# Second products of MoE1 by Strassen's method, with partial sums seeded in PSUM

## The chip, the cores and the metric

The kernel runs on one core of a Trainium2 chip. The core has a matrix engine (TensorE, PE in the rows), a vector engine (VectorE, DVE), an activation engine (ScalarE, ACT), GpSimd (POOL) and SyncE (SP); SP and POOL issue the DMAs here. Operands lie in SBUF, matmuls write into eight PSUM banks. The metric is the device time of one execution in microseconds (us), as the median of several.

## What is computed

```python
kv = einsum('bhsd,bhse->bhde', k, v); out = einsum('bhsd,bhde->bhse', q, kv)
x = out / sqrt(mean(out*out, -1) + 1e-6) * g_norm     # 4608 tokens x 512
r = maximum(x @ w_in, 0); x = (s * (r*r) + b) @ w_out   # MoE1: 512 -> 2048 -> 512
h = x @ w2_in; y = (h / (1 + exp(-1.702*h))) @ w2_out   # MoE2, same sizes
```

All of it is float32.

## The kernel before, in words

The 4608 tokens are nine blocks of T = 512. Every float32 product is made of three matmuls with operands split into a high and a low part (`w` into wh and wl, an activation into xh and xl or gh and gl): wh·xh, wh·xl, wl·xh. A matmul is 128x128 weights on 128x512 values. The low parts are differences on VectorE (`x_lo`, `mlp_g`, `g2_lo`, `go_lo`), the high parts copies on ScalarE.

MoE1 (`m = 0`) does blocks 0 to 2 plainly, interleaved with attention and the preparation of the weights. Then come three pairs of blocks, (3,4), (5,6) and (7,8). Their first products (x @ w_in) go by Strassen's method in Winograd's form: the weights and activations are quartered, and seven products of quarters or sums of quarters replace eight (`first_products`: eight groups of seven products, six matmuls in a product, 336 matmuls). The weight sums (S1 to S4 beside A11 to A22, `OPS`) are made once and kept in DRAM. The second products of these pairs are plain (`second_plain`: 384 matmuls at L569). MoE2 (`m = 1`) has four such pairs, with Strassen's method for both products, and a last plain block.

Products are summed thus in a group (`g1_product`, `g1_sum`): the first goes into PSUM bank a; ScalarE copies it to SBUF (L628); VectorE adds the product in b to the copy (L631), then the one in c (L635), and takes from these the quarters r of the result, with the product in d (L638) and so on: five adds a group. The fifth product goes on in bank a, the seventh in bank d after L638 has read it. Then r is squared (MoE1) or gated: ScalarE makes a sigmoid, VectorE multiplies (L649, L650). MoE1 scales r by s and adds b (`g2_scale`, L670) before it is split.

The order of every engine's instructions is written by hand: `at(slot, fn, ...)` puts a step at a time slot (twelve matmuls, 2.72 us), all steps are sorted by slot, and each step emits its instructions on whatever engines it uses. `attend` is the attention of a block, `x_operands` and `x_sub` (L506) the sums of activations, `w_join`, `s_sums` (L267 to L270), `op_hi`, `op_lo` (L283) and `op_store` the preparation of weight sums.

Of the kernel before, what the change touches and what calls it, by code (L numbers as in the profile page):

```python
# [27 lines left out]
KV = ((-0.5, 2.5), (24.5, 28), (34, 41), (46, 57), (62.5, 66.5), (74, 79), (84, 89))  # L28
# [4 lines left out]
ATT = ((1.5, 2.5, 3.3), (40, 3.5, 4.8), (55, 4, 4.8), (67, 4, 4.8))  # L33
LEAD_G = 3.9
SIDE = (0, 0, 0, 1, 2, 0, 0, 0, 0, 2, 0, 1, 1, 1, 1, 2)
# [49 lines left out]
LEAD = 4  # L85
LAG = 2
G1_ACT = (0, 0, 0, 1.5, 0.2, 1.6, 1.6)
OPS = ("A11", "S2", "S3", "S1", "A12", "A22", "S4", "A21")
PRODUCTS = (("A11", "B11"), ("S2", "T2"), ("S3", "T3"), ("S1", "T1"), ("A12", "B21"), ("A22", "T4"), ("S4", "B22"))

# [17 lines left out]
def kernel(ctx: ExitStack, tc: tile.TileContext, q_h, kv_h, kt, vt, cst,  # L108
# [15 lines left out]

    def new(slots, shape, dtype, name):
        t, n = slots.take(shape, dtype, name)
        where[id(t)] = (slots, n, t)
        return t

    def drop(*tiles):  # L130
        for t in tiles:
            slots, n, _ = where.pop(id(t))
            slots.give(n)
# [6 lines left out]

    def psum(name):
        return new(bank, [P, T], F32, name)
# [6 lines left out]
    g_col = cp.tile([P, 1], F32, name="g_col")  # L149
    eps = cp.tile([P, 1], F32, name="eps")  # L150
# [20 lines left out]
    raws, vals, W = {}, {}, {}  # L171

    def w_load(m, f, which):
        raw = new(big, [P, 512, 2], U32, "raw")
        src = w_raw[m][which]
        nc.sync.dma_start(out=raw.rearrange("p c t -> p (c t)"), in_=src[f * P:(f + 1) * P, :])
        raws[m, f, which] = raw
# [37 lines left out]
    wod = [dp.tile([P, 2, 512], F32, name=f"wod{f}") for f in range(NF)]  # L215
    wsd = [[dp.tile([P, len(OPS), 512], F32, name=f"wsd{m}_{i}") for i in range(NF // 2)] for m in range(2)]
    wo2 = [dp.tile([P, NF // 2, 512], F32, name=f"wo2{name}") for name in OPS]

    def op_place(m, i, which, name):
        return wo2[OPS.index(name)][:, i, :] if which else wsd[m][i][:, OPS.index(name), :]  # L220
# [6 lines left out]
    def wo_store(f):  # L227
        pool.dma_start(out=wod[f], in_=W[0, f, 1].bitcast(F32))

    def wo_load(m, f):  # L230
        w = W[m, f, 1] = new4(F32R, "w")
        if m == 0:
            nc.sync.dma_start(out=w.bitcast(F32), in_=wod[f])
        else:
            for a, name in enumerate(OP_PAIRS[1][f % 2]):
                nc.sync.dma_start(out=w[:, a, :].bitcast(F32), in_=op_place(m, f // 2, 1, name))

    def a_store(f):
        w = W[0, f, 0]
        for c, name in enumerate(OP_PAIRS[0][f % 2]):  # L240
            pool.dma_start(
                out=op_place(0, f // 2, 0, name).rearrange("p (h c) -> p h c", h=2),
                in_=w[:, :, c * 256:(c + 1) * 256].bitcast(F32),
            )

    def w_join(f):
        w = W[0, f, 0]
        q = vals[0, f, 0] = new2(U32, "ca")
        dve.tensor_add(out=q.bitcast(F32), in0=w[:, 0, :].bitcast(F32), in1=w[:, 1, :].bitcast(F32))

        w_spent(f)
# [3 lines left out]
    def w_spent(f):  # L255
        if f in spent:
            drop(W.pop((0, f, 0)))
        spent.add(f)
# [165 lines left out]
    def att_copy(j, p):  # L424
        o_ps, sq = att[j, p]
        o = new2(F32, "oc")
        dve.tensor_copy(out=o, in_=o_ps)
# [69 lines left out]
    def x_lo(src, key, last):  # L497
        hi, lo = xop[key]
        dve.tensor_sub(out=lo, in0=xin[src], in1=hi.bitcast(F32))
        if last:  # L500
            drop(xin.pop(src))
# [9 lines left out]
    def mlp_h(m, j, f, first=0, last=NP):  # L511
# [16 lines left out]
        elif j == NPLAIN - 1:  # L528
            w_spent(f)
# [4 lines left out]
    def mlp_act(m, j, f):  # L534
# [5 lines left out]
        else:  # L540
            act.activation(r, h, AF.Sigmoid, scale=1.702)
            dve.tensor_mul(out=r, in0=h, in1=r)
# [29 lines left out]
    def wo_done(m, f):  # L572
        drop(W.pop((m, f, 1)))
# [25 lines left out]
    def g1_product(m, i, k):  # L599
        op, xname = PRODUCTS[k]  # L600
        n = OPS.index(op)
        w = wl[m, i, n // 2][:, n % 2, :]
        x = xop[m, xname]
# [10 lines left out]
        if k in (1, 3, 5, 6):  # L614
            drop(wl.pop((m, i, {1: 0, 3: 1, 5: 2, 6: 3}[k])))
        if i == NF // 2 - 1 and k == 6:
            for _, name in PRODUCTS:
                drop(*xop.pop((m, name)))

    def r_half(q, i):  # L620
        if i % 2 == 0:
# [3 lines left out]
    def g1_sum(m, i, k):  # L625
        if k == 0:
            st["c1"] = new2(F32, "c1")
            act.activation(st["c1"], st[0], AF.Copy)  # L628
        elif k == 1:
            st["u2"] = new2(F32, "u2")  # L630
            dve.tensor_add(out=st["u2"], in0=st[1], in1=st["c1"])  # L631
            drop(st.pop(1), st.pop("c1"))
        elif k == 2:
            st["u3"] = new2(F32, "u3")
            dve.tensor_add(out=st["u3"], in0=st[2], in1=st["u2"])  # L635
            drop(st.pop(2))
        elif k == 3:
            dve.tensor_add(out=r_half("22", i), in0=st[3], in1=st["u3"])  # L638
        elif k == 5:
            dve.tensor_add(out=r_half("21", i), in0=st[5], in1=st["u3"])  # L640
            drop(st.pop(5), st.pop("u3"))
        elif k == 6:
            dve.tensor_add(out=r_half("12", i), in0=st[6], in1=st["u2"])
            drop(st.pop(6), st.pop("u2"))
            del st[3]

    def gate(r, h):
        t = new2(F32, "t")
        act.activation(t, h, AF.Sigmoid, scale=1.702)  # L649
        dve.tensor_mul(out=r, in0=h, in1=t)  # L650
        drop(t)

    def g1_act(m, i, k):
        if k == 4:
            r = r_half("11", i)
            if m == 0:
                act.activation(r, st[4], AF.Relu)
            else:
                gate(r, st[4])
            drop(st.pop(4))  # L660
            del st[0]
        elif m == 1 and k in (3, 5, 6):
            r = R[{3: "22", 5: "21", 6: "12"}[k], i // 2][:, i % 2, :]
            gate(r, r)

    def r_act(q, n, fn):
        act.activation(R[q, n], R[q, n], fn)  # L667

    def g2_scale(q, n):
        act.activation(R[q, n], R[q, n], AF.Identity, scale=s_col, bias=b_col)  # L670

    def quarter(f, n):
        return ("11", "12", "21", "22")[f % 2 * 2 + n], f // 4, f // 2 % 2

    def g2_hi(m, j, f, n):
        gh, gl = G[m, j, f] = new2(F32R, "gh"), new2(F32R, "gl")
        q, i, half = quarter(f, n)
        act.activation(gh, R[q, i][:, half, :], AF.Copy)  # L678

    def g2_lo(m, j, f, n):  # L680
        gh, gl = G[m, j, f]
        q, i, half = quarter(f, n)
        dve.tensor_sub(out=gl, in0=R[q, i][:, half, :], in1=gh.bitcast(F32))  # L683
        if half:
            drop(R.pop((q, i)))


# [3 lines left out]
    def t_sums(n):  # L691
        t = new4(F32, "t1")
        dve.tensor_sub(out=t, in0=R["12", n], in1=R["11", n])
        dve.tensor_sub(out=R["12", n], in0=R["22", n], in1=t)
        drop(t)
# [384 lines left out]
```

## Time and profile before

| | |
|---|---|
| median of 3 timed runs | 1547.94 us (1547.73 to 1550.01) |
| profiled execution, its own time | 1547.51 us |
| its span, first to last instruction | 1545.6 us |
| TensorE busy | 1530.0 us, 99% |
| VectorE, ScalarE busy | 1062.7 us (69%), 789.6 us (51%) |
| moved by DMA | 392.11 MB, mean 254 GB/s |

The profiled execution is one run with timestamps for each instruction. Busy shares are means over all stages; the stages of the pairs lie, in us from the span's start: pair (3,4) first products 334.7 to 420.9, second 420.9 to 507.9; pair (5,6) 508.0 to 593.8 and to 680.8; pair (7,8) 680.9 to 757.0 and to 844.0; then MoE2, each stage 76 us.

### The profile page before, as it was taken

What the parts mean: (1) busy time and instruction counts of PE and PEld (TensorE: products, weight loads), DVE (VectorE), ACT (ScalarE), POOL (GpSimd) and SP (SyncE); (2) the same over time, 40 slices, a digit from 0 to 9 for tenths busy, and PEclk for the clock granted to TensorE, in tenths of its full rate; (3) what the DMA queues carried; (4) which work ended last, traced back from release to release, by engine and by line L of the source; (5) the groups of instructions that cost most, each with busy time, mean ns of one, the idle gap of its engine ahead of it and who ended that gap; (6) DMA issues with size and microseconds to landing.
All of it is one profiled execution on the core that took longest, in us unless ns stands there. A gap on an engine that the chain in (4) does not pass through costs nothing.

```text
span 1545.6 us, 20632 instructions
## 1 busy us (share of the span) xinstructions
PE 1530.0 (99%) x7368; PEld 1238.4 (80%) x7368; DVE 1062.7 (69%) x1535; ACT 789.6 (51%) x1169; POOL 232.6 (15%) x424
## 2 busy tenths in 40 slices
PE   8999999999999999999999999999999999999998
PEld 5788777877788778888888888888888888888887
DVE  5996366577885677847661889688958795788422
ACT  5997454445893569826871245323522453244221
POOL 1101425512421333221201000000000000000000
PEclk9999999999999999999999999999999999999999
DMA  9635568897896989778865737974797479347930
GB/s 356 206 99 212 197 226 299 281 401 269 305 390 235 325 300 374 273 282 286 295 226 171 249 114 276 357 275 139 266 365 258 148 260 378 126 168 235 374 122 28
DMA packets 125270, 392.11 MB, mean 254 GB/s; under 512 B 17008, under 2 KB 17136, under 8 KB 125168
## 3 DMA queue, kind: packets, MB, share of 16 engines
q1 hardware_dynamic: 93664, 289.18, 53.2%
q0 software_dynamic: 31504, 101.61, 17.8%
q8 instruction: 59, 0.97, 0.2%
q14 instruction: 43, 0.35, 0.1%
HBM read 300.42 MB, written 90.31 MB: 253 GB/s over the span
## 4 chain that ended last, share of the span: by engine, by line
issue 50%; PE 36%; ACT 4%; DMA 4%; POOL 3%; DVE 3%; SPq 0%; POOLq 0%; ACTq 0%; DVEq 0%
PE o L569 18%; PE h L522 6%; PE d L612 3%; PE a L612 3%; PE c L612 1%; PE b L612 1%; PE f L612 1%; POOL out L593 1%; ACT r L667 1%; DMA raw<-in_w_in 1%; DMA kv_in<-in_kv 1%; PE kv L350 1%; PE o_ps L381 1%; DMA qq<-in_q 1%; DMA x0d<-oc 1%
## 5 line engine op out<-in xcount | busy, mean ns | idle before, releaser
L569 PE MATMUL o<-gh,w 128*128 128x512 f32 x1280 | 404.7, 390 | 0.0
L569 PEld LDWEIGHTS o<-gh,w 128*128 128x128 f32 x1280 | 240.2, 188 | 53.8 <-issue 4.0
L740 PE MATMUL o<-gh,wl 128*128 128x512 f32 x896 | 276.5, 389 | 0.0
L569 PE MATMUL o<-gl,w 128*128 128x512 f32 x640 | 249.0, 389 | 0.0
L740 PEld LDWEIGHTS o<-gh,wl 128*128 128x128 f32 x896 | 168.2, 188 | 34.9
L740 PE MATMUL o<-gl,wl 128*128 128x512 f32 x448 | 174.3, 389 | 0.0
L522 PE MATMUL h<-xh,w 128*128 128x512 f32 x512 | 170.7, 395 | 1.9 <-DVE w L211 1.1
L612 PE MATMUL d<-xh,wl 128*128 128x512 f32 x448 | 156.9, 391 | 3.5 <-DVE r L638 3.5
L612 PE MATMUL a<-xh,wl 128*128 128x512 f32 x448 | 156.6, 390 | 0.0
L569 PEld LDWEIGHTS o<-gl,w 128*128 128x128 f32 x640 | 120.1, 188 | 24.5
L522 PEld LDWEIGHTS h<-xh,w 128*128 128x128 f32 x512 | 96.2, 188 | 29.7 <-issue 5.0
L628 ACT ACTIVATE c<-a 128x512 f32<-128x512 f32 x56 | 33.4, 597 | 163.0 <-PE a L612 160.1
L593 POOL DMA_DIRECT2D out<-st x36 | 19.6, 544 | 591.0 <-DVE st L762 467.4
L612 PEld LDWEIGHTS d<-xh,wl 128*128 128x128 f32 x448 | 84.1, 188 | 23.5 <-DVE r L638 5.1
L522 PE MATMUL h<-xl,w 128*128 128x512 f32 x256 | 100.3, 392 | 0.2 <-DVE xl L481 0.2
L612 PEld LDWEIGHTS a<-xh,wl 128*128 128x128 f32 x448 | 84.1, 188 | 20.2 <-issue 2.8
L740 PEld LDWEIGHTS o<-gl,wl 128*128 128x128 f32 x448 | 84.1, 188 | 17.5
L683 DVE TENSOR_TENSOR gl<-r,gh 128x512 fp32r<-128x512 f32 x96 | 65.0, 687 | 33.2 <-ACT gh L678 16.5
L612 PE MATMUL d<-xl,wl 128*128 128x512 f32 x224 | 87.2, 389 | 0.0
L612 PE MATMUL a<-xl,wl 128*128 128x512 f32 x224 | 87.2, 389 | 0.0
L667 ACT ACTIVATE r<-r 128x1024 f32<-128x1024 f32 x84 | 84.5, 1052 | 0.0
L714 ACT ACTIVATE gh<-t 128x1024 fp32r<-128x1024 f32 x48 | 51.0, 1062 | 63.7 <-DVE t L705 58.1
(129 smaller groups left out, 2778.7 us busy)
## 6 DMA issues: line engine op xcount, KB each, us to landing
wl<-wsd SPq DMA_DIRECT2D x168, 512.0 KB, 6.4
wl<-wo2S SPq DMA_DIRECT2D x64, 512.0 KB, 6.2
wsd<-op POOLq DMA_DIRECT2D x96, 256.0 KB, 4.6
w<-wod SPq DMA_DIRECT2D x48, 512.0 KB, 8.1
wl<-wo2A SPq DMA_DIRECT2D x48, 512.0 KB, 4.5
kv_in<-in_kv SPq DMA_DIRECT2D x32, 512.0 KB, 5.7
raw<-in_w_in SPq DMA_DIRECT2D x32, 512.0 KB, 7.9
raw<-in_w_out SPq DMA_DIRECT2D x32, 512.0 KB, 6.2
```

What stands on the lines that cost most here:

```text
L350: pe.matmul(kv[r:r + D, p // 2, h * D:(h + 1) * D], lhsT=kt_, rhs=vt_, start=(p in (opens, opens + 1) and h == 0 and c == 0), stop=False, ...
L381: pe.matmul(att[j, p][0][h * D:(h + 1) * D, o:o + n], lhsT=kvs[b % 4][r:r + D, p // 2, h, :], rhs=qin[j, p // 2][r:r + D, h, o:o + n], sta ...
L522: pe.matmul(h, lhsT=a, rhs=b, start=(n == 0), stop=(n == 3 * NP - 1))
L569: pe.matmul(acc[m, j][c], lhsT=a, rhs=x, start=(f == 0 and n == 0), stop=(f == NF - 1 and n == 2))
L593: pool.dma_start(out=out[c * P:(c + 1) * P, j * T:(j + 1) * T], in_=t)
L612: pe.matmul(o, lhsT=a, rhs=b, start=(first and n == 0), stop=(n == 5), skip_group_check=not first)
L628: act.activation(st["c1"], st[0], AF.Copy)
L667: act.activation(R[q, n], R[q, n], fn)
L683: dve.tensor_sub(out=gl, in0=R[q, i][:, half, :], in1=gh.bitcast(F32))
L714: act.activation(hi, src, AF.Copy)
L740: pe.matmul(so[k, d], lhsT=a, rhs=b, start=(first and n == 0 and i == 0 and e == 0), stop=(n == 3 and i == 1 and e == 2), skip_group_check ...
```

## The change

1. The second products of MoE1's three pairs are done by the method that MoE2 uses (`second_products(0, ...)`, 336 matmuls). The sums of W_out's quarters are prepared and stored like those of W_in. The scale s is applied when results leave PSUM, and b as a constant per output row, b times the column sums of W_out (`col_add`, `col_sums`: four matmuls of one column); `g2_scale` is gone for the pairs.
2. In both MoEs partial sums are formed in PSUM. ScalarE copies a finished bank into another bank (`g1_copy`, `g2_seed`: ub from pa, uc from ub, ob from oa, oc from ob), and matmuls go on accumulating on it without a start flag. pd is copied to SBUF by ScalarE. Two VectorE adds a group remain. `psum()` gives a seed only a bank that matmuls have filled whole. The order of products follows (`G1_PLACE`, `G1_FIRST`, `G2_ORDER`).
3. MoE2's gate is one activation (`Gelu_apprx_sigmoid`) instead of sigmoid and product.
4. Attention's copies out of PSUM (`att_copy`) go to ScalarE for all blocks but 1.
5. The slots (`ATT`: start of a block's attention, gap, and when its scaling begins; `G2`: how many slots ahead of a product its weights are loaded, its sums formed and split) of attention, weights and sums are other numbers (`KV`, `ATT`, `GROUPS`, `SUMS`, `X0`, ...), and all groups of W2_in are prepared before those of W2_out. When the middle-sized tiles run out, a big one is halved.

```diff
-ATT = ((1.5, 2.5, 3.3), (40, 3.5, 4.8), (55, 4, 4.8), (67, 4, 4.8))
+ATT = ((1.5, 2.5, 3.3), (40, 3.5, 4.8), (55.977, 2.5, 5.138), (67, 3.698, 4.378))
...
+G2 = (4.012, 3.247, 2.887, 1.879)
+G2_ORDER = (0, 3, 1, 4, 2, 6, 5)
...
+G1_PLACE = (0, 3, 6, 5, 8, 9, 11)
+G1_FIRST = (0, 2, 6, 1, 3, 9, 11)
...
     def g1_product(m, i, k):
...
-        first = k not in (4, 6)
-        st[k] = psum("abcdefg"[k]) if first else st[0 if k == 4 else 3]
-        o = st[k]
+        if k in (0, 3):
+            st[i, "pa" if k == 0 else "pd"] = psum("pa" if k == 0 else "pd")
+        o = st[i, ("pa", "ub", "uc", "pd", "pa", "uc", "ub")[k]]
...
-                pe.matmul(o, lhsT=a, rhs=b, start=(first and n == 0), stop=(n == 5), skip_group_check=not first)
+                pe.matmul(o, lhsT=a, rhs=b, start=(k in (0, 3) and n == 0), stop=(n == 5), skip_group_check=k not in (0, 3))
...
+    def g1_copy(i, k):
+        if k == 3:
+            t = new2(F32, "c4")
+            act.activation(t, st[i, "pd"], AF.Copy)
+            drop(st[i, "pd"])
+            st[i, "pd"] = t
+            return
+        src, name = (("pa", "ub"), ("ub", "uc"))[k]
+        st[i, name] = psum(name)
+        act.activation(st[i, name], st[i, src], AF.Copy)
+
+    def g1_sum(i, q):
+        a = st[i, "uc" if q == "22" else "ub"]
+        dve.tensor_add(out=r_half(q, i), in0=st[i, "pd"], in1=a)
...
+        act.activation(r, src, AF.Gelu_apprx_sigmoid if m else AF.Relu)
...
+    def g2_seed(k, d):
+        src, name = (("oa", "ob"), ("ob", "oc"))[k]
+        so[name, d] = psum(name)
+        act.activation(so[name, d], so[src, d], AF.Copy)
...
+            act.activation(t, o, AF.Identity, scale=s_col, bias=cb[:, half + d:half + d + 1])
...
+                dve.scalar_tensor_tensor(out=t, in0=o, scalar=s_col, in1=u, op0=ALU.mult, op1=ALU.add)
...
-        base = second_plain(j, seconds[0, j])
+        base = second_products(0, j, seconds[0, j])
...
-        base = second_products(j, seconds[1, j])
+        base = second_products(1, j, seconds[1, j])
```

What stands in an engine's queue at three places, before and after. First ScalarE where the first products of pair (3,4) begin, before (L582 stores the last plain block, L628 is the copy of a's product, L182 and L183 convert MoE2's weights, L390 squares attention):

```order
L582 ACTIVATE st<-o 128x512 x2
L628 ACTIVATE c_3369<-a 128x512
L182 ACTIVATE ca<-raw 128x512
L183 ACTIVATE cu<-raw 128x512
L657 ACTIVATE r<-a 128x512
L182 ACTIVATE ca<-raw 128x512
L183 ACTIVATE cu<-raw 128x512
L390 ACTIVATE sq<-o_ps 128x512 x2
```

The same place in the change (L713 writes a seed, L707 copies pd, L725 takes r out of PSUM, L348 and L234 are weights, L460 attention):

```order
L658 ACTIVATE st<-o 128x512 x2
L348 ACTIVATE op<-s_3506 128x2x256
L348 ACTIVATE op<-s_3507 128x2x256
L713 ACTIVATE ub<-pa 128x512
L707 ACTIVATE c_3585<-pd 128x512
L713 ACTIVATE uc<-ub 128x512
L725 ACTIVATE r<-pa 128x512
L713 ACTIVATE ub<-pa 128x512
L234 ACTIVATE ca<-raw 128x512
L235 ACTIVATE cu<-raw 128x512
L725 ACTIVATE r<-uc 128x512
L460 ACTIVATE sq<-o_ps 128x512
```

Three copies from PSUM stand where one stood, two of them with ub or uc, PSUM banks, as the target.

Second VectorE at the end of the preparation, before (L499 is a low part of an activation operand, L506 a difference of operands, L283 a low part of a weight sum, L631 to L638 the adds of the first group):

```order
L499 TENSOR_TENSOR xl<-x,xh 128x1024
L554 TENSOR_SCALAR g<-r,cst_sb 128x512
L559 TENSOR_TENSOR gl<-g,gh 128x512
L283 TENSOR_TENSOR op<-s_3213,op 128x2x256
L499 TENSOR_TENSOR xl<-x,xh 128x1024
L506 TENSOR_TENSOR x<-x 128x1024
L499 TENSOR_TENSOR xl<-x,xh 128x1024
L580 COPY st<-o 128x512 x2
L499 TENSOR_TENSOR xl<-x,xh 128x1024
L631 TENSOR_TENSOR u_3373<-b,c_3369 128x512
L635 TENSOR_TENSOR u_3395<-c,u_3373 128x512
L638 TENSOR_TENSOR r<-d,u_3395 128x512
```

The same place in the change (L572 and L580 are now the operands, L299 joins a weight of W_out, L337 to L340 sum it, L313 adds to its column sums, L717 is the add of r22):

```order
L337 TENSOR_TENSOR s_3506<-ca 128x256
L338 TENSOR_TENSOR s_3507<-ca 128x256
L339 TENSOR_TENSOR s_3506<-s_3506,ca 128x256
L340 TENSOR_TENSOR s_3507<-ca,s_3506 128x256
L313 TENSOR_TENSOR cs<-cs,s_3506 128x256
L313 TENSOR_TENSOR cs<-cs,s_3507 128x256
L572 TENSOR_TENSOR xl<-x,xh 128x1024
L656 COPY st<-o 128x512 x2
L353 TENSOR_TENSOR op<-s_3506,op 128x2x256
L353 TENSOR_TENSOR op<-s_3507,op 128x2x256
L572 TENSOR_TENSOR xl<-x,xh 128x1024
L717 TENSOR_TENSOR r<-c_3585,uc 128x512
```

W_out's sums stand between the last operands, and of the first group's adds one follows where three did.

Third VectorE in the second stage of pair (3,4), before (L683 makes gl for the plain products, 512 elements wide; L189 to L196 convert weights):

```order
L683 TENSOR_TENSOR gl<-r,gh 128x512
L506 TENSOR_TENSOR x<-x 128x1024
L683 TENSOR_TENSOR gl<-r,gh 128x512
L283 TENSOR_TENSOR op<-s_4373,op 128x2x256
L683 TENSOR_TENSOR gl<-r,gh 128x512 x3
L189 TENSOR_SCALAR cu<-cu 128x512
L190 TENSOR_SCALAR cu<-cu 128x512
L499 TENSOR_TENSOR xl<-x,xh 128x1024
L195 SCALAR_TENSOR_TENSOR cu<-raw,cu 128x512
L196 ISA ca<-cu,ca 128x1024
L683 TENSOR_TENSOR gl<-r,gh 128x512
```

and in the change (L760 forms a sum of results, L776 its low part, both 1024 wide):

```order
L776 TENSOR_TENSOR gl<-r,gh 128x1024
L353 TENSOR_TENSOR op<-s_4718,op 128x2x256
L760 TENSOR_TENSOR t<-r 128x1024
L776 TENSOR_TENSOR gl<-t,gh 128x1024
L353 TENSOR_TENSOR op<-s_4719,op 128x2x256
L760 TENSOR_TENSOR t<-r 128x1024
L776 TENSOR_TENSOR gl<-t,gh 128x1024
L572 TENSOR_TENSOR xl<-x,xh 128x1024
L760 TENSOR_TENSOR t<-r 128x1024
L776 TENSOR_TENSOR gl<-t,gh 128x1024
L580 TENSOR_TENSOR x<-x 128x1024
L776 TENSOR_TENSOR gl<-t,gh 128x1024
```

The differences are twice as wide and have sums of results between them.

## Rows read from the trace of the kernel before

**Rows 1.** The page, busy us, share of the span and instructions of each engine.

```profile
PE 1530.0 (99%) x7368; PEld 1238.4 (80%) x7368; DVE 1062.7 (69%) x1535; ACT 789.6 (51%) x1169; POOL 232.6 (15%) x424
```

**Rows 2.** Windows by stage: length, busy us (instructions) of PE, PEld, DVE, ACT, POOL; clock, DMA share, GB/s.

```profile
334.70:420.90 86.20, 84.24 (x417) 64.83 (x417) 64.22 (x111) 55.64 (x83) 25.69 (x47) 1.00 0.87 305
420.90:507.90 87.00, 87.00 (x385) 72.03 (x385) 59.66 (x97) 61.22 (x88) 18.61 (x35) 1.00 0.84 307
508.00:593.80 85.80, 84.31 (x401) 64.17 (x400) 63.89 (x109) 54.08 (x81) 29.60 (x55) 1.00 0.93 321
844.00:920.20 76.20, 76.20 (x338) 63.10 (x337) 58.32 (x81) 25.68 (x44) 3.78 (x7) 1.00 0.55 189
```

**Rows 3.** Waits of TensorE: engine, tile, line, releaser: total us, times, longest us.

```profile
PE d L612 <- DVE r L638: 3.5, 4, 1.3
PE ms L396 <- ACT sq L390: 2.6, 3, 2.0
```

**Rows 4.** Timeline of TensorE, pair (3,4): start us, length us, instruction [idle before].

```profile
335.89 0.39 PE L612 MATMUL a<-xh,wl 128*128 128x512 f32 x1
...
341.56 0.39 PE L612 MATMUL f<-xh,wl 128*128 128x512 f32 x1
...
353.46 0.39 PE L612 MATMUL f<-xh,wl 128*128 128x512 f32 x1
355.19 0.50 PE L612 MATMUL d<-xh,wl 128*128 128x512 f32 x1 [1.34 <-DVE r L638]
```

**Rows 5.** Timeline of VectorE at the first of these waits.

```profile
352.98 0.41 DVE L267 TENSOR_TENSOR s<-ca 128x256 f32<-128x256 f32 x1
353.32 0.42 DVE L268 TENSOR_TENSOR s<-ca 128x256 f32<-128x256 f32 x1
...
354.45 0.68 DVE L638 TENSOR_TENSOR r<-d,u 128x512 f32<-128x512 f32 x1
355.05 0.68 DVE L283 TENSOR_TENSOR op<-ca,op 128x512 fp32r<-128x512 f32 x1
```

**Rows 6.** Groups by line: engine, operation, tiles, shapes, count | busy us, mean ns | idle before.

```profile
L714 ACT ACTIVATE gh<-r 128x1024 fp32r<-128x1024 f32 x64 | 65.5, 1051 | 0.0
L650 DVE TENSOR_TENSOR r<-r,t 128x512 f32<-128x512 f32 x96 | 65.2, 683 | 0.1
...
L628 ACT ACTIVATE c<-a 128x512 f32<-128x512 f32 x56 | 33.4, 597 | 163.0 <-PE a L612 160.1 <-issue 3.0
...
L189 DVE TENSOR_SCALAR cu<-cu 128x512 f32<-128x512 f32 x64 | 27.3, 426 | 8.9 <-ACT cu L183 8.7
```

**Rows 7.** Timeline of ScalarE where the first products of pair (3,4) begin.

```profile
336.32 0.60 ACT L628 ACTIVATE c<-a 128x512 f32<-128x512 f32 x1 [1.20 <-PE a L612]
336.81 0.65 ACT L182 ACTIVATE ca<-raw 128x512 uint32<-128x512 uint32 x1
```

**Rows 8.** DMA in the window 420.9 to 507.9: 40 slices; totals; loads, KB, us to landing.

```profile
GB/s 267 403 388 305 340 406 411 411 407 405 414 416 401 420 420 407 405 397 337 305 350 85 0 299 288 316 298 294 220 256 308 413 414 154 0 115 247 0 299 258
DMA packets 8227, 26.71 MB, mean 307 GB/s; under 512 B 1078, under 2 KB 1078, under 8 KB 8221
...
w<-wod SPq DMA_DIRECT2D x13, 512.0 KB, 8.9
```

**Rows 9.** Timeline of VectorE at the end of the preparation.

```profile
310.68 2.48 DVE L506 TENSOR_TENSOR x<-x 128x1024 f32<-128x1024 f32 x2 [5.41 <-DMA x<-x0d]
...
316.82 1.22 DVE L499 TENSOR_TENSOR xl<-x,xh 128x1024 fp32r<-128x1024 f32 x1
317.96 0.69 DVE L249 TENSOR_TENSOR ca<-w 128x512 f32<-128x512 f32 x1
...
326.49 0.69 DVE L559 TENSOR_TENSOR gl<-g,gh 128x512 fp32r<-128x512 f32 x1 [0.49 <-ACT gh L552]
...
335.57 1.22 DVE L499 TENSOR_TENSOR xl<-x,xh 128x1024 fp32r<-128x1024 f32 x1
```

More of the change, by code (lines that the diff above doesn't have):

```diff
@@ L123 @@
     where = {}
+    halves = []
     def new(slots, shape, dtype, name):
+        if slots is mid and not mid.free:
+            if not halves:
+                t, n = big.take([P, 2, T], F32, "halves")
+                halves.extend((t, n, a) for a in range(2))
+            whole_tile, n, a = halves.pop(0)
+            t = whole_tile[:, a, :]
+            if dtype != F32:
+                t = t.bitcast(dtype)
+            where[id(t)] = (halves, (whole_tile, n, a), t)
+            return t
         t, n = slots.take(shape, dtype, name)
@@ L132, in drop @@
             slots, n, _ = where.pop(id(t))
-            slots.give(n)
+            if slots is not halves:
+                slots.give(n)
+                continue
+            other = [h for h in halves if h[1] == n[1]]
+            if other:
+                halves.remove(other[0])
+                big.give(n[1])
+            else:
+                halves.append(n)
     def new4(dtype, name):
@@ L139, in new2 @@
         return new(mid, [P, T], dtype, name)
+    whole = set()
     def psum(name):
+        if name in ("ub", "uc", "ob", "oc"):
+            n = next(n for n in bank.free if n in whole)
+        else:
+            n = next((n for n in bank.free if name in PARTIAL and n not in whole), bank.free[0])
+        bank.free.remove(n)
+        bank.free.insert(0, n)
+        (whole.discard if name in PARTIAL else whole.add)(n)
         return new(bank, [P, T], F32, name)
@@ L225, with wo_load @@
     )
[L227 to L240, printed above, removed]
+    def wo_load(f):
+        w = W[1, f, 1] = new4(F32R, "w")
+        for a, name in enumerate(OP_PAIRS[1][f % 2]):
+            nc.sync.dma_start(out=w[:, a, :].bitcast(F32), in_=op_place(1, f // 2, 1, name))
@@ L249, in w_join, with col_add @@
         dve.tensor_add(out=q.bitcast(F32), in0=w[:, 0, :].bitcast(F32), in1=w[:, 1, :].bitcast(F32))
-        w_spent(f)
+        w_spent(f, which)
+    col = {}
+    def col_add(i):
+        s12, s34 = sums[0, i, 1]
+        if i == 0:
+            col["sum"] = new2(F32, "cs")
+        for out, part in ((slice(256, 512), s12[:, :256]), (slice(0, 256), s34[:, 256:])):
+            o = col["sum"][:, out]
+            if i == 0:
+                dve.tensor_copy(out=o, in_=part)
+            else:
+                dve.tensor_add(out=o, in0=o, in1=part)
@@ L253, with col_sums, w_spent @@
+    def col_sums():
+        t, ps = col.pop("sum"), psum("cs")
+        dve.tensor_add(out=t[:, :256], in0=t[:, :256], in1=t[:, 256:])
+        for c in range(NP):
+            pe.matmul(ps[:, c:c + 1], lhsT=t[:, c * P:(c + 1) * P], rhs=ones_1, start=True, stop=True)
+        dve.tensor_scalar(out=cb, in0=ps[:, :NP], scalar1=b_col, scalar2=None, op0=ALU.mult)
+        drop(t, ps)
     spent = set()
[L255 to L258, printed above, removed]
+    def w_spent(f, which):
+        if (f, which) in spent:
+            drop(W.pop((0, f, which)))
+        spent.add((f, which))
@@ L666, in r_act @@
     def r_act(q, n, fn):
+        assert n not in T1 and count[q, n] == 2 + (fn == AF.Square and q in ("22", "12"))
+        count[q, n] += 1
         act.activation(R[q, n], R[q, n], fn)
[L669 to L685, printed above, removed]
+        if fn == AF.Square:
+            ready.add((q, n))
+            del count[q, n]
     GOP, so = {}, {}
     def t_sums(n):
-        t = new4(F32, "t1")
+        t = T1[n] = new4(F32, "t1")
+        assert all((q, n) in ready for q in ("11", "12", "22"))
         dve.tensor_sub(out=t, in0=R["12", n], in1=R["11", n])
@@ new lines, in first_products @@
+        for i in range(n):
+            first = base + 3.5 * i + min(shift, 7 * i // 2)
+            for k in range(4):
+                at(first + 0.5 * min(G1_PLACE[e] for e in range(7) if OPS.index(PRODUCTS[e][0]) // 2 == k) - LEAD, op_load, m, i, k)
+            if i % 2:
+                for (q, k, fn), t in zip(() if m else R_STEPS, R_T):
+                    at(place[i, k] + t, r_act, q, i // 2, fn)
+                at(place[i, 6] + T_SUMS[m], t_sums, i // 2)
+        return base + 28 + shift
```

361 lines of the change are left out of this document (188 added, 173 removed).

## The prediction

> **What bounds the kernel now.** I read the busy shares first [rows 1]: TensorE is busy for 99% of the span, VectorE 69%, ScalarE 51%. The time is thus the number of matmuls times their pace, plus the moments at which TensorE waits. The table by stage gives the pace [rows 2]: the 87.00 us of one pair's plain second products hold 384 matmuls, 0.2266 us each; the 76.20 us of a MoE2 pair's first products hold 336, 0.2268 each; neither has a pause, and the granted clock is 1.00, the upper level of 2.4 GHz. A matmul removed from the second products of MoE1 is therefore worth 0.2267 us, provided that what feeds TensorE keeps up.
>
> TensorE's waits come next [rows 3]: the largest of eight rows is 3.5 us, in four waits for the add in L638; the others come to 7 us, at the kernel's start and for attention, and none of them names a gl, a weight load after the start, or a transfer of a second stage. The timelines show one of them. The last matmul into f starts at 353.46, the next one, into d, only at 355.19 [rows 4]: 1.73 us later instead of 0.23. L638 has to read the bank of d first; it starts at 354.45, behind four weight sums that VectorE's order puts ahead of it from 352.98 on [rows 5]. The row shows 1.34 us idle; 0.16 us of overlap between neighbours is lost besides, 1.50 us in all. So the four cost 3.5 + 4 x 0.16 = 4.1 us. In the first second stage VectorE is busy 59.66 of 87.00 us, ScalarE 61.22 [rows 2]; there is room, and the question is how much of it the change uses.
>
> **What the change removes.** Each of three pairs does its second products in 336 instead of 384 matmuls: 144 x 0.2267 = **-32.6 us**. The waits for L638 hang on an edge that is gone: before, the seventh product went on in d after VectorE had read it; now d is read once, by ScalarE, and its bank given back: **-4.1 us**. Four matmuls of one column are new (the column sums of W_out). No row has their like; the nearest is a 512-column matmul, so they cost 0 to 4 x 0.23 = 0.9 us. I take 0.3, low because of the one column.
>
> **ScalarE: the seeds.** For each group of seven first products it now copies twice from PSUM to PSUM and once from PSUM to SBUF (once before), and for each pair's second products it writes four seeds. That it writes PSUM is not in the trace. The nearest row is L628's copy out of PSUM, 0.597 us [rows 6]; the bounds are the step from that copy to the next instruction, 0.49 us [rows 7], and twice the row, 1.2 us; I take 0.6, the same copy with another place to write. Does TensorE wait for it? The last matmul of a's first product starts at 335.89 and lasts 0.39 us [rows 4]; the copy starts at 336.32 [rows 7], 0.04 us after its end. A seed written so is there at 336.92, 0.80 us after the next product began (336.12). By the order of the change two products, 12 x 0.2267 = 2.72 us, lie between a bank's product and the product on its copy, and only one, 1.36 us, at the very start of a stage. So ScalarE may be 1.9 us late, or 0.56 us at the start. Two activations of 1024 elements, 1.05 us each [rows 6], ahead of a seed use that up. In pair (3,4), ScalarE's list in the first products grows from 45 instructions of 512 elements to 76, at 0.5 us a step +15 us, to 71 of about 83 us [rows 2]; there I take **1 us** of waits (0 to 2). In MoE2 it is busy for 25.68 of 76.20 us [rows 2] and gets about 10 more; I take nothing (0 to 0.5).
>
> **VectorE.** It loses three of five adds in each group, the 144 multiplications by the sigmoid (0.683 us each [rows 6], off TensorE's path in [rows 3], so worth nothing by themselves), and most attention copies. In MoE1's second stages it gains: 28 differences gl of 1024 elements replace 32 of 512, and eight sums come on top. By the order the first such stage has 46 instructions of 1024 elements, 23 of the length of a 512-element one, ten scalar ones and eight of 256. At the steps of the timelines (1.14 us [rows 9], 0.60 and 0.34 [rows 5]) and 0.43 for the scalar ones [rows 6]: 46 x 1.14 + 23 x 0.60 + 10 x 0.43 + 8 x 0.34 = 73 us of the 76.2 that TensorE needs; in the two later ones 70 and 67. At 96% every wait of VectorE for a load becomes lateness. I take **1.5 us** for the first (0 to 5) and **0.5** for the others together (0 to 3).
>
> The end of the preparation is the other crowded place. From 310.68, where it had waited 5.41 us for a load, VectorE runs to 336.8 with no wait above 0.49 us [rows 9]. In this stretch stand the operands of the first Strassen products, the last gl of the plain blocks and weight sums. The xl that ends at 336.79 belongs to the sixth product, which starts at 341.56 [rows 4]: 4.8 us are left. The order shows W_out's weight and column sums in this stretch too: from the first x_sub to the last xl the list takes 33 us of steps instead of 25. Against these 8 us: the last attention block is scaled 0.72 slots of 2.72 us earlier, 2.0 us; the product stands one place later, 1.4 us; and the 4.8 us left. That cancels for the xl itself; but right behind it stands the add of r22, which must have read uc before the A22 product writes on in it. I take **3 us** (1 if the load lands early, 6 if the first x_sub starts no sooner and the add is late with the xl).
>
> **Transfers.** By the order the first second stage of MoE1 now issues 28.6 MB in 76.2 us, 375 GB/s; the window of before carried 26.71 MB in 87.00 us [rows 8] at a share of 0.84 [rows 2]. Yet a dozen of that window's slices in a row stand at 401 to 420 GB/s [rows 8], and TensorE waits for no load in it [rows 3]; I put nothing here (0 to the 12 us of rival c). The Trainium skill ("DMA: Bandwidth & Descriptors", Where 436 GB/s comes from) says that about 358 GB/s binds between HBM and SBUF; by it this stage takes an estimated 80 us and the sum rises by 4 us. The slices at 420 GB/s do not agree with that limit.
>
> **Sum**, against the profiled execution's own 1547.51 us: -32.6 - 4.1 + 0.3 + 1 + 1.5 + 0.5 + 3 = -30.4, so 1517.1. The median of the timed runs lies 0.4 us above that execution: **1517.5 us**.
>
> **Rivals.**
> (a) *Nearly no waits*: the lists are full but nothing is late, 1517.5 - 6 = 1511.5. For it: TensorE waits for no gl in the trace [rows 3]. Against it: 73 of 76.2 us.
> (b) *VectorE becomes the bound* at the end of the preparation and in the second stages: the upper ends 6 + 5 + 3 and 2 for the seeds, 16 instead of 6, 1527.5. For it: the 96%, and a wait like the 5.41 us that may come anywhere. Against it: in the first products VectorE's list falls to 45 to 52 us of 76, so that lateness is made good there.
> (c) *Transfers bind.* The 321 GB/s from 508.00 on came at a share of 0.93 [rows 2]; at full share that is 345 GB/s. The first second stage (28.6 MB) and the first products after it (28.1 MB, by the order) then last 83 and 81 us instead of 76: +12, 1529.5. For it: that row, and weight loads that land after 8.9 us [rows 8] where they are issued four slots, 10.9 us, ahead. Against it: 420 GB/s in the same trace. The Trainium skill's 358 GB/s is this rival at a third of the price.
> (d) *Seeds on the path, slower than before.* MoE1's 48 seeds in first products, where ScalarE is fullest, decide from 36.4 / 48 = 0.76 us each: ScalarE would have to be 1.9 + 0.76 = 2.7 us late each time, five queued copies. At 1 us each the time is 1511.5 + 48 = 1559.5. For it: 71 of 83 us. Against it: ScalarE's list is shorter than the stage, so lateness does not add up from group to group.
>
> **Chances.** Forecast 0.57, (a) 0.16, (b) 0.13, (c) 0.09, (d) 0.05; the last with 0.03 above the time before and 0.02 near it. A difference of 3 us, 0.2%, is about what a measurement of this kernel tells from none. So faster 0.95, same 0.02, slower 0.03. The forecast's own terms span 1513 to 1523; for 8 in 10 the range takes in (a) and reaches to (b): 1511 to 1528.
>
> **What would show it.** Right: the second stages of the three pairs 76 to 78 us long; no wait for d; waits of TensorE of 1 to 4 us in all within 15 us after the first Strassen product begins, released by VectorE (an xl or the add of r22); few and short waits for ScalarE's copies. Wrong: second stages of 80 us with a DMA share near 1 and loads as releasers (c); gl as releaser all through them (b); a wait for ub, uc, ob or oc in every group (d). A single long wait for a load at a stage's start, as at 310.68 but with TensorE behind it, would put me out by its length.

## The result and the profile after

The changed kernel takes 1523.36 us (median; 1521.08 to 1524.03) against 1547.84 us: a ratio of 0.9837 (95% interval 0.9820 to 0.9854), 24.5 us faster. Forecast were 1517.5 us and a range of 1511 to 1528; the time lies in it, 5.9 us above the forecast. The profiled execution took 1524.03 us, the longest of the four runs.

The stages, to be held against [rows 2] (windows: length, busy us and instructions of PE, PEld, DVE, ACT, POOL; clock, DMA share, GB/s). The first two are pair (3,4), then the second stages of (5,6) and (7,8), then MoE2's first:

```profile
336.50:430.10 93.60, 87.03 (x426) 66.53 (x425) 59.26 (x97) 75.37 (x119) 30.58 (x57) 0.98 0.92 327
430.10:508.10 78.00, 78.00 (x337) 64.14 (x336) 74.71 (x88) 49.22 (x61) 12.39 (x23) 0.98 0.95 349
591.80:668.00 76.20, 76.20 (x338) 63.11 (x337) 70.68 (x79) 50.88 (x62) 7.57 (x15) 1.00 0.92 331
744.10:820.30 76.20, 76.20 (x338) 63.07 (x337) 70.83 (x80) 50.50 (x61) 7.56 (x14) 1.00 0.87 318
820.30:896.50 76.20, 76.20 (x338) 63.10 (x337) 27.06 (x32) 39.95 (x65) 7.52 (x14) 1.00 0.75 282
```

Two second stages last 76.2 us where 87.0 stood, with VectorE busy for 71 us and TensorE never waiting. The first lasts 78.0 us, and its clock column reads 0.98, as does that of the stage before it, which is 7.4 us longer than before (93.60 for 86.20). TensorE's waits, against [rows 3] (releaser: total us, times, longest us):

```profile
PE ub L689 <- DMA wl<-wsd: 5.4, 1, 5.4
PE ms L466 <- ACT sq L460: 2.6, 3, 1.9
PE o L642 <- DVE gl L632: 2.3, 2, 1.7
...
PE kv L420 <- ACT oc L500: 1.3, 1, 1.3
...
PE ub L689 <- ACT ub L713: 0.4, 1, 0.4
PE pa L689 <- DMA wl<-wsd: 0.4, 1, 0.4
PE uc L689 <- ACT uc L713: 0.3, 1, 0.3
```

The waits for the add into r are gone. In their place stands one wait of 5.4 us for a weight load, the last of pair (3,4)'s first products, and 2.3 us for gl at the end of the preparation. TensorE's timeline around the long wait shows a second loss behind it:

```profile
421.79 0.39 PE L689 MATMUL uc<-xh,wl 128*128 128x512 f32 x1
427.56 0.79 PE L689 MATMUL ub<-xh,wl 128*128 128x512 f32 x1 [5.38 <-DMA wl<-wsd]
...
433.27 0.63 PE L798 MATMUL oa<-gl,wl 128*128 128x512 f32 x1
433.69 0.67 PE L798 MATMUL oa<-gh,wl 128*128 128x512 f32 x2
```

The matmuls from 427.56 to 433.27 follow each other at 0.43 us, not 0.227: the granted clock is 0.50 there (window 427.5 to 433.3), the lower level of 1.2 GHz, for 14 matmuls, about 3.1 us. The column sums cost 0.8 us, from the start of their first instruction to the next product, since each of the four matmuls stands in the trace as two instructions:

```profile
362.92 0.95 PE L319 MATMUL cs<-ones,cs 128*128 128x1 f32 x8
363.73 0.49 PE L689 MATMUL uc<-xh,wl 128*128 128x512 f32 x1
```

The time, step by step from the profile of before (differences of starts beyond 0.227 us): -32.6 for matmuls, -4.1 for L638; +2.6 for gl, +1.1 for two seeds, +6.1 for two weight loads, +3.1 for the clock, +0.8 for the column sums, +0.9 for the attention's copy at 262 us: -22.1. The two profiled executions differ by 23.5; the 1.4 us between lie in many small differences at the start and in the attention and are not assigned further.

Why was the load late? SyncE's queue, in the window 395 to 432:

```profile
SPq L786 <- DMA wsd<-op: 13.3, 3, 9.9
SPq L371 <- DMA wsd<-op: 7.4, 1, 7.4
```

The wait of 9.9 us ends with the first of these two issues of SyncE, and the load comes right behind it:

```profile
420.70 0.32 SPq L786 DMA_DIRECT2D wl<-wo_A  x1
421.12 0.40 SPq L371 DMA_DIRECT2D wl<-wsd  x1
```

So the load (L371) was issued only at 421.12, and it took 6.4 us to land; SP stood 9.9 us before a load of the second products (L786), whose tile came free when a weight store had landed. Two theories follow. **Queue:** the order in SP's and POOL's queues put the load behind a store. **Transfers:** the DMA engines are full there, store and loads alike land late, and another order moves the wait only.

### The profile page after: what moved, and what is told of

Read it like the earlier page. It is cut to its first block, busy times and chain, and to the rows that moved or that the text cites. A ratio compares the mean times of both kernels' runs of the same rounds, so it can differ in the third digit from the quotient of the medians.

```text
span 1522.2 us, 20253 instructions
## 1 busy us (share of the span) xinstructions
PE 1500.6 (99%) x7232; PEld 1214.9 (80%) x7232; DVE 944.1 (62%) x1273; ACT 890.7 (59%) x1325; POOL 252.6 (17%) x457
## 4 chain that ended last, share of the span: by engine, by line
issue 45%; PE 38%; DVE 5%; DMA 5%; ACT 4%; POOL 3%; SPq 0%; POOLq 0%; DVEq 0%; ACTq 0%
PE oa L798 4%; PE ob L798 4%; PE ub L689 4%; PE h L596 4%; PE uc L689 4%; PE pa L689 4%; PE o L642 4%; PE oc L798 4%; PE od L798 2%; PE pd L689 2%; POOL out L669 1%; DMA wl<-wsd 1%; DMA yb<-yd 1%; DMA x<-x1d 1%; DVE ca L299 1%
## 5 line engine op out<-in xcount | busy, mean ns | idle before, releaser
L642 PE MATMUL o<-gh,w 128*128 128x512 f32 x512 | 168.2, 392 | 0.0
L717 DVE TENSOR_TENSOR r<-c,ub 128x512 f32<-128x512 f32 x56 | 38.5, 687 | 200.5 <-PE ub L689 200.5
L689 PE MATMUL uc<-xh,wl 128*128 128x512 f32 x448 | 156.8, 391 | 0.3 <-ACT uc L713 0.3
L689 PE MATMUL ub<-xh,wl 128*128 128x512 f32 x448 | 149.6, 392 | 5.8 <-DMA wl<-wsd 5.4
L689 PE MATMUL pa<-xh,wl 128*128 128x512 f32 x448 | 150.4, 391 | 0.4 <-DMA wl<-wsd 0.4
L776 DVE TENSOR_TENSOR gl<-r,gh 128x1024 fp32r<-128x1024 f32 x112 | 134.8, 1218 | 20.9 <-ACT gh L771 20.9
L798 PE MATMUL oa<-gh,wl 128*128 128x512 f32 x448 | 141.4, 392 | 0.0
L798 PE MATMUL ob<-gh,wl 128*128 128x512 f32 x448 | 140.2, 389 | 0.0
L798 PE MATMUL oc<-gh,wl 128*128 128x512 f32 x448 | 140.2, 389 | 0.0
L776 DVE TENSOR_TENSOR gl<-t,gh 128x1024 fp32r<-128x1024 f32 x84 | 101.4, 1218 | 21.5 <-ACT gh L771 21.3
L642 PEld LDWEIGHTS o<-gh,w 128*128 128x128 f32 x512 | 96.1, 188 | 23.2 <-issue 3.0
L642 PE MATMUL o<-gl,w 128*128 128x512 f32 x256 | 99.9, 390 | 2.3 <-DVE gl L632 2.3
```

Of the source, the lines that this page charges most:

```text
L642: pe.matmul(acc[m, j][c], lhsT=a, rhs=x, start=(f == 0 and n == 0), stop=(f == NF - 1 and n == 2))
L689: pe.matmul(o, lhsT=a, rhs=b, start=(k in (0, 3) and n == 0), stop=(n == 5), skip_group_check=k not in (0, 3))
L717: dve.tensor_add(out=r_half(q, i), in0=st[i, "pd"], in1=a)
L776: dve.tensor_sub(out=lo, in0=src, in1=hi.bitcast(F32))
L798: pe.matmul(so[name, d], lhsT=a, rhs=b, start=(k in (0, 3) and n == 0 and i == 0 and e == 0), stop=(n == 3 and i == 1 and e == 2), skip_gr ...
```

## The experiments

Ratios are to the kernel before, run beside each; the kernel that is edited is the changed one. Most edits change one thing; 6 joins two, and 8 puts several things back together.

**1. The last weight loads ahead** (`last_load_ahead`).

```diff
-... - LEAD, op_load, m, i, k)
+... - LEAD - (2 if i == NF // 2 - 1 and k >= 2 and not m and base == 32 * NPLAIN else 0), op_load, m, i, k)
```

> In the first products of pair (3,4) the last two weight loads (wl<-wsd of group 8) are issued two slots earlier, ahead of the loads of the second products; nothing else moves. Queue theory: the load came 5.4 us late because it stood in SP's queue behind a load whose tile was not free until a weight store had landed (SP waited 9.9 us there). Then the wait of ub for it is gone, the clock stays at 1.00 in the next ten us, and the time falls from 1523.4 by 5.5 + 3.1 us to 1514.8 (1513.5 to 1516.5). Transfer theory: the load was late because the DMA engines were full (share 0.92); then a wait of 3 us or more for a weight load stays, here or a product later, and the time is 1519 to 1523.4.

1524.57 us, ratio 0.9844 (0.9830 to 0.9857): no gain. The wait for the load is gone, and TensorE stands 2.7 us for the seed of uc instead, since ScalarE's queue now holds the instruction that waits for the same store (timeline of ScalarE):

```profile
420.66 0.63 ACT L348 ACTIVATE op<-s 128x512 fp32r<-128x512 f32 x1 [4.98 <-DMA wsd<-op]
421.20 0.58 ACT L713 ACTIVATE uc<-ub 128x512 f32<-128x512 f32 x1
```

The time is above both forecasts. The queue theory falls in its simple form: another place for the load ends its own wait and gains nothing. The wait of 3 us or more for a weight load that the transfer theory forecast did not come either. What both kernels share is a store that lands at 420.6.

**2. The wait filled** (`gap_filled`).

```diff
+        if (m, i, k) == (0, NF // 2 - 1, 6) and not fills:
+            t = psum("spare")
+            for _ in range(20):
+                pe.matmul(t, lhsT=x[0][:, 0, :P], rhs=x[0][:, 0, :], start=True, stop=True)
```

> Twenty matmuls that nobody reads (a spare bank) are put in TensorE's queue just before the product that waits 5.4 us for its weights; the load is as late as before. Clock theory: the fourteen matmuls after the wait took 0.43 us instead of 0.227 because the granted clock fell to its lower level after TensorE had idled for 5.4 us; with 4.5 us of the wait filled it stays at 1.00, and the time falls from 1523.4 by about 3.1 us to 1520.3 (1519.5 to 1521.2). Rival: they were slow for another reason (operands or banks still being written, the transfers beside them); then they stay at 0.43 us and the time stays at 1523.4 (1522.8 to 1524.5).

1522.33 us, 0.9826 (0.9812 to 0.9839); the profiled execution took 1519.69. Its timeline of TensorE:

```profile
421.04 4.70 PE L688 MATMUL spare<-xh 128*128 128x512 f32 x20
425.57 0.39 PE L698 MATMUL ub<-xh,wl 128*128 128x512 f32 x1
425.80 0.39 PE L698 MATMUL ub<-xl,wl 128*128 128x512 f32 x1
```

The product on ub goes on at 0.23 us: the clock theory holds for this place, in the profile. The load was a little less late than before, issued at 419.53 instead of 421.12, so that about 4 us of wait were filled and not 5.4; a wait of 3.9 us did bring the lower clock in experiment 6. The median gained 1.0 us, not 3.1, and lies between the forecasts. The unprofiled executions report mean clocks of 0.997 to 0.998 against 0.999 in the profiled one, so something in them was still slow; no record shows where.

**3. W_out's last sums later** (`wout_sums_later`).

```diff
-            slot = SUMS[which][0] + SUMS[which][1] * i
+            slot = SUMS[which][0] + SUMS[which][1] * i + (4 if which and i > 5 else 0)
```

> The joins, sums and column sums of the last two groups of W_out are made four slots (10.9 us) later, out of the end of the preparation. Crowding theory: the two waits for gl there (1.84 and 0.77 us) come from these sums on VectorE; they go, and with them the 0.6 us wait for the first ub; the time falls by 2.6 to 3.2 us to 1520.2 to 1520.8 if the late load stays as it is. Rival: VectorE is late there because of the loads of x, and the work moved only delays the first products: the gl waits stay at 2 us or more, or as much comes back as waits for adds into uc; 1522.5 to 1525.

1521.99 us, 0.9828 (0.9815 to 0.9841). Both waits for gl are gone, but the wait of the first ub for ScalarE has grown from 0.4 to 1.7 us and one for the add of r22 has come (waits of TensorE from 300 to 440 us):

```profile
PE ub L689 <- DMA wl<-wsd: 4.2, 1, 4.2
PE ub L689 <- ACT ub L713: 1.7, 1, 1.7
PE uc L689 <- DVE r L717: 1.7, 1, 1.7
```

The wait for the add of r22 is the one that the prediction had named; the sums do cause the crowding, but later they crowd the next place, and the time lies between the two forecasts.

**4. Block 2's copies back on VectorE** (`copy_back_j2`): `COPY = (1, 2)`.

> Only block 2's attention copies go back from ScalarE to VectorE. If the 1.3 us wait of a kv product for ScalarE's copy (at 262 us) comes from that move, it shrinks to the 0.5 us that stood there before or goes, and the time falls by 0.5 to 1.5 us (1522 to 1523); if VectorE's crowding at the end of the preparation is what matters, nothing falls and the gl waits grow (1523.4 to 1525).

1523.10 us, 0.9835 (0.9821 to 0.9848). The wait at 262 us is absent from the profile, but so it is from that of `gap_filled`, where nothing of the kind was changed, so it varies from run to run. One wait for gl, of 2.0 us, is left where there were two (1.7 and 0.6), and 7 matmuls behind it ran at the lower clock; but kernels that leave this part alone have waits of 1.1 us (`seeds_twice`) to 2.1 us (`gap_filled`) there, so this is no effect of the edit that can be told. The gain is below 1 us, not told from none.

**5 and 6. Block 6's attention earlier**, alone (`y6_earlier`) and with edit 1 (`y6_and_load`).

```diff
-ATT2 = (((5.181, 4.812, 5.534), (14.855, 4, 6.776)), ...
+ATT2 = (((5.181, 4.812, 5.534), (12.855, 4, 8.776)), ...
```

> The attention of block 6 up to the loads of its broadcast factor (yb) is done two slots (5.4 us) earlier; its scaling stays where it was. Store theory: what held SP in the change, and ScalarE when the two weight loads were moved ahead, is one tile that is free only when a weight store (wsd) has landed at 420.6; that store was issued between 411 and 414 behind eight yb loads in POOL's queue and landed right after the last of them. With those gone 5 us earlier the store lands by 416, SP issues the last wl load by 417, the 5.4 us wait shrinks to 1 us or less and the clock holds: 1514.5 to 1517.5. Rival: the transfers are slow in this stretch whatever comes first; the store lands after 419 and the time is 1521.5 to 1524.5.

> Both moves together: block 6's attention two slots earlier and the last two weight loads of pair (3,4) ahead of the second products' loads. Store theory: with the store landing by 416 neither SP nor ScalarE is held; no wait over 1 us at the end of the first products, clock 1.00 there, 1513.5 to 1516. Rival (slow transfers): a wait for the same store stays with ScalarE, as when the loads alone were moved (2.7 us and a lower clock): 1521 to 1525.

1520.43 us, 0.9817 (0.9803 to 0.9831), and 1523.12 us, 0.9837 (0.9823 to 0.9851). The first lies between the forecasts, the second in the rival's. In the first kernel the wait for the last load is gone and the clock holds at 421 us; these two waits stand in its list:

```profile
PE o L642 <- DVE gl L632: 2.5, 2, 2.1
PE pa L689 <- DMA wl<-wsd: 1.7, 1, 1.7
```

SP's queue moved as the store theory says, only less: the store lands at 418.4 instead of 420.6, and the last load is issued at 418.95 instead of 421.12. The 1.7 us are for the load before it, issued at 411.58 and 10.4 us under way. Behind the 2.1 us for gl the granted clock fell, which it had not done at that place in the changed kernel, and some 1.7 us were lost there.

In the second kernel the loads of the last group are issued at 405 to 411, and TensorE still waits 3.9 us, because they are under way for 10.7 us, the one it waits for from 406.51 to 419.93 (DMA of 400 to 420 us: share and GB/s in 40 slices; loads, KB, us to landing):

```profile
DMA  9999999999899998899999999999999999999999
GB/s 401 410 451 402 401 434 410 418 393 434 254 295 279 287 238 229 279 279 320 344 295 238 270 262 352 426 393 426 418 418 406 389 393 418 430 402 430 410 426 426
...
wl<-wsd SPq DMA_DIRECT2D x2, 512.0 KB, 10.7
wsd<-op POOLq DMA_DIRECT2D x4, 256.0 KB, 8.6
```

The engines are full from end to end, at 229 to 451 GB/s. That is the transfer theory, and rival (c) of the prediction, one stage earlier than it was put. So both theories hold a part: in the changed kernel the last load is late because it is issued late, behind a late store, and with the queue out of the way the transfers themselves are too slow.

**7. Each MoE2 seed twice** (`seeds_twice`): a second `act.activation` on the same bank in `g1_copy`, in MoE2.

> Each of MoE2's 64 PSUM-to-PSUM copies in the first products is done twice by ScalarE, the second time with the same data. Slack theory: ScalarE may be 1.9 us late with a seed and one copy more is 0.5 to 0.6 us, so the MoE2 stages stay at 76 us and the time at 1523.4 (1522.5 to 1524.5). Rival (seeds on the path): each repeat delays the product on it, 64 x 0.5 = 32 us, 1550 to 1560; a part of it, if only some seeds are tight.

1526.20 us, 0.9855 (0.9840 to 0.9870), above the slack theory's forecast. A MoE2 first stage takes 77.0 us for 76.2; in all four stages weight loads of TensorE waited 5.1 us in pieces of up to 0.3 us:

```profile
PEld ub L689 <- ACT ub L715: 3.7, 11, 0.3
PEld uc L689 <- ACT uc L715: 1.4, 4, 0.3
```

Of the 32 us of a seed on the path, some 3 came: most seeds have the slack that was worked out, a quarter have less than 0.6 us of it.

**8. First products summed on VectorE again** (`first_sums_on_vector`): `g1_product`, `g1_sum` and the order of products of before, the rest as changed, `NBIG, NMID = 42, 23`.

> The first products of both MoEs are summed as before the change (one ScalarE copy to SBUF and five VectorE adds a group, products in the order 0 to 6), with 42 and 23 tiles instead of 41 and 25; everything else, the second products by Strassen's method among it, stays as changed. If the seeds took the four waits for the add on d away and nothing else, those come back, one to six of them, 4 us, and the waits at the transition stay: 1524 to 1529. Rival: VectorE, with 24 adds or 15 us more in each first stage, becomes the bound in MoE1's pairs, where its list is 67 to 75 us in the second stages: waits for gl and xl all through, 1535 or more.

1537.83 us, 0.9928 (0.9915 to 0.9942), 14.5 us above the changed kernel.

```profile
PE d L689 <- DVE r L717: 9.9, 4, 6.1
PE kv L420 <- ACT oc L500: 4.2, 1, 4.2
```

The time is the rival's, but not its mechanism: no wait for gl or xl runs all through. The waits on d are back and larger, all in MoE1, and the longest brought the lower clock with it (13 matmuls); MoE2's stages stay at 76 us. The 4.2 us before the pairs may come from the smaller pool of tiles. Without them some 10 us are left, more than the 4.1 us of these waits in the old schedule. The slots were not fitted again for VectorE's adds, so what the seeds are worth against a schedule made for the other way is not shown.

**9. One weight group moved** (`group3_moved`): `GROUPS[3]` from 116.047 to 250.3.

> One group of MoE2's weights (two loads of 512 KB, eight stores of 256 KB, 3.1 MB, and its sums) is prepared in the second stage of pair (7,8) instead of the first products of pair (3,4); no other step moves. Transfer theory: there the DMA engines are full between 400 and 422 us, so that loads issued in time take 10 to 13 us; 3.1 MB less is some 9 us of transfers. The 5.4 us wait for the last wl shrinks to under 1 us, the clock holds, and the time is 1513.5 to 1517, if VectorE's second stage of pair (7,8), 70.8 us before and about 77 then, gives no more than 1 us back. Rival: it is the order in SP's and POOL's queues alone and another load or store takes this one's place: a wait of 3 us or more at 410 to 425, 1520 to 1524.

1522.92 us, 0.9832 (0.9819 to 0.9846); the profiled execution took 1521.01. At 421 us TensorE no longer waits for anything, and the first products of pair (3,4) are 7.6 us shorter. But the second stage of pair (7,8), now with 77.2 us of VectorE, takes 81.0 us instead of 76.2 and gives more than half of it back in the profiled execution; the median gained 0.4 us (window of that stage, then its wait):

```profile
736.20:817.20 81.00, 78.06 (x337) 64.10 (x337) 77.16 (x92) 54.97 (x69) 11.85 (x22) 0.98 0.91 331
...
PE oc L798 <- DVE gl L776: 2.9, 1, 2.9
```

with 8 matmuls at the lower clock behind it. Both terms that the prediction weighed are real: VectorE binds in a second stage as soon as 6 us of work are added to it, and the wait at 421 us hangs on what is moved in that stretch. The group took its stores out of POOL's queue as well as its bytes out of the engines, so this run does not tell the queue from the transfers.

**10. Fewer broadcasts** (`fewer_broadcasts`).

```diff
+        if j == 6 and p:
+            att[j, p] = (att[j, p][0], att[j, 0][1])
+            return
         y = new2(F32, "yb")
```

> Six of the eight broadcast loads (yb) of block 6 are left out, so that three quarters of that block are scaled by another head pair's factor; everything else stays. They are 0.75 MB, 2.2 us of transfers at 345 GB/s, but while they run the slices show a full share at 60 to 240 GB/s. If they cost the engines by their bytes alone, the wait of 5.4 us for the last wl falls by 2.2 us at most and the time to 1521 to 1522.5. If they cost them three times that, as those slices suggest, the wait all but goes and the clock holds: 1514.5 to 1517.

1518.34 us, 0.9808 (0.9795 to 0.9822), between the two forecasts. TensorE's waits for weight loads at the end of the first products fall from 5.8 to 1.0 us, by 4.8 us where the bytes take 2.2, and the clock holds there:

```profile
PE pa L693 <- DMA wl<-wsd: 0.6, 1, 0.6
PE ub L693 <- DMA wl<-wsd: 0.4, 1, 0.4
```

Two waits of 1.8 and 1.1 us are new in the second stage (446 to 451 us). In the changed kernel the share and the GB/s of 404 to 420 us read

```profile
DMA  9999899984137789938999977979999899999997
GB/s 379 415 379 440 333 394 379 379 328 174 72 123 225 164 266 246 174 133 307 328 338 225 123 102 133 215 215 338 277 348 266 246 369 399 420 410 410 410 430 297
```

with several slices of share 9 at 123 to 246 GB/s between 410 and 414 us, where the broadcasts are under way. So they cost more than their bytes. Both ways show in the last load: without the six it is issued at 418.22 instead of 421.12, 2.9 us sooner, since the store frees SP's tile sooner, and it is 4.6 us under way instead of 6.4. That the store itself is sooner because it stands behind fewer loads in POOL's queue, or because the engines are freer, was not separated.

**11. Sigmoid and product again** (`sigmoid_product`): MoE2's gate as before the change.

> MoE2's gate is again a sigmoid on ScalarE and a product on VectorE, 144 products more (99 us of VectorE's time); everything else stays as changed. If that part of the change lies off TensorE's path, as argued, the time stays at 1523.4 within 1.5 us. Rival: TensorE's waits in MoE2 are absent only because VectorE has 47 to 52 us of 76 there; with 20 us more in the first products, sums come late for the second ones and MoE2's stages grow by 1 us or more each, 1528 or above.

1526.02 us, 0.9854 (0.9839 to 0.9867), between the forecasts. MoE2's first stages take 76.7 to 77.2 us instead of 76.2, 3.4 us together (waits of TensorE's weight loads in MoE2):

```profile
PEld uc L690 <- DVE r L718: 5.5, 17, 0.6
```

The A22 product on uc waits for the add of r22, and that add stands behind the products of the gate. I had put this part at nothing; with the new edge it is worth some 3 us.

**12. Two weight groups spread** (`groups_spread`): in `GROUPS`, W2_in's groups 0 and 3 take the places 228.87 and 221.15 of W2_out's groups 5 and 4, which go to 280 and 272, into MoE2's first stage.

> Two of MoE2's sixteen weight groups leave the crowded stretch: group 0 of W2_in (end of the plain blocks) and group 3 (first products of pair (3,4)) take the places of two groups of W2_out in the first products of pair (7,8), and those two are prepared in MoE2's first stage, where VectorE has 28 of 76 us. VectorE's list loses 8 us before and 8 us in the first products of pair (3,4), and the second stages keep theirs. Theory: the 2.6 us for gl, the 0.6 us for the first ub, the 6.1 us for weight loads and the 3.1 us of lower clock all come from these two crowded places and go; MoE2's first stage gives at most 1 us back. 1523.4 - 12.4 + 0.5 = 1511.5 (1510 to 1514.5). Rival: work that is moved takes the wait along, as with W_out's sums and with group 3 alone; waits of 4 us or more appear elsewhere in MoE1, 1517 to 1522.

1515.13 us (1514.34 to 1517.94), 0.9787 (0.9774 to 0.9801): faster than both kernels, 8.2 us below the change and 0.6 us above the forecast's range. There is no wait for a weight load, no wait for a gl before the pairs and, between the kernel's start and its end, no stretch at the lower clock. Besides waits in the kernel's first 80 us the largest that are left are

```profile
PE uc L689 <- DVE r L717: 1.6, 1, 1.6
...
PE kv L420 <- ACT oc L500: 0.7, 1, 0.7
PE od L798 <- DVE gl L776: 0.5, 1, 0.5
...
PE oc L798 <- DVE gl L776: 0.4, 1, 0.4
...
PE uc L689 <- ACT uc L713: 0.3, 1, 0.3
```

the first of them in MoE2's stage to which the groups went.

## Why the prediction was right, and where not

The gain came as forecast, and the time lies in the range; that it does is in part luck. The range had been drawn up to 1528 for rival (b), VectorE, and the 5.9 us above the forecast came by (c), transfers. Of the signs that were named, second stages of 76 to 78 us and no wait for d came true. The 1 to 4 us of waits for VectorE just after the first Strassen product did not: VectorE's waits, for gl, lie at 325 to 331 us, before that product. The long single wait for a load that was named last came, at a stage's end and not at its start. Term by term:

- *The matmuls, -32.6 us, and L638, -4.1 us*: as forecast. The stages of 76.2 us show the first, the list of waits the second.
- *Column sums, 0.3 us*: 0.8 us. They are eight instructions in the trace, not four.
- *ScalarE's seeds, 1 us in MoE1*: two waits of 0.6 and 0.5 us. Rival (d) is out: of 48 seeds in MoE1 two were waited for. In MoE2 ScalarE's list grew by 14.3 us a first stage (39.95 for 25.68) and not by 10, and nothing waited; even a second copy costs 0.05 us a seed on average (7).
- *The end of the preparation, 3 us*: 2.6 us, but at gl, before the first Strassen product, not at the xl or the add of r22 behind it. Experiment 3 shows that the add comes next.
- *VectorE in the second stages, 2 us*: 0 in the profiled execution. 0.5 us at the same places in several of the experiments; a wait of 2.9 us when 6 us of work are added (9).
- *Transfers, nothing*: **this is the term that was mis-sized.** It measured 6.1 us of waits and 3.1 us of clock, 9.2 together; with the other terms (VectorE -2.0, preparation -0.4, seeds +0.1, column sums +0.5, attention's copy +0.9 and the -1.4 that are not assigned) 6.9 us, and the profiled execution lies 6.9 us above the sum of 1517.1. The step that failed has two parts. The sum had no term for a load that is issued late: SP stood 9.9 us before a tile that a store still held, and the load behind it landed 5.4 us too late. And I had taken slices of 401 to 420 GB/s in the old second stage as what the engines can do anywhere. In the first products of pair (3,4) the same full share carries 123 to 246 GB/s in slices while the broadcasts run (10), and there the change adds its stores and the next stage's loads. The trace of before has such slices too, in a stage that the prediction did not read for this: 236 to 256 GB/s at a share of 9 from 413.6 to 415.2 us. How much of the 9.2 us is the queue's and how much the engines' stays open; experiments 6 and 10 show both. The Trainium skill's limit of 358 GB/s ("DMA: Bandwidth & Descriptors", Where 436 GB/s comes from) does not describe it either: slices of 410 to 430 GB/s stand beside the wait (10), the wait arose in a stage that moved 327 GB/s on average, and the second stage, for which the prediction's estimate by that limit was 80 us, took 78.0 with no wait for a load.
- The price of a wait was also too low: the stop of 5.4 us cost its length and 3.1 us at the lower clock behind it.

## What to carry to other kernels

When a change shortens a stage, add up what its engines and queues must carry per microsecond in the stage before it as well, since the loads for the short stage are issued there. A full DMA share is no rate: read the GB/s beside it, by what is being moved. And where two stages are crowded, move work to the stage with the lowest sum, not to the next one: sums moved a little later took their waits along (3), a group moved into a stage that VectorE already filled made a new wait there (9), and two groups moved to where VectorE and the engines had room were worth 8 us (12).

## What was not expected of the hardware

After the kernel's first 60 us, the granted clock fell to its lower level after every single wait of TensorE of 2.7 us or more but one: after 5.4 us in the changed kernel, with 14 matmuls at 0.43 us, after 2.7 us for ScalarE (1) with 13, after 2.9 us for VectorE (9) with 8, and not after 2.8 us for VectorE in experiment 8, at 602 us. After the wait of 2.0 to 2.1 us for gl at 324 to 329 us it fell in four kernels (`copy_back_j2`, with 7 matmuls, `y6_earlier`, `y6_and_load`, `fewer_broadcasts`) and held in four (`gap_filled`, `last_load_ahead`, `group3_moved`, `sigmoid_product`); after waits of 1.8 us or less it held in all. So between 2.0 and 2.8 us the length of a wait alone did not tell. With the wait filled by matmuls (2) the clock held. The Trainium skill ("TensorE: Matmul & The Clock Gate", HAM oscillation — how this bites in real kernels) says that waits for DMA bring the lower clock; the traces agree, and show it after waits for VectorE and ScalarE too.
